# Splitting a small weight load, trimming warm-up matmuls and moving a loop's entry waits, in a matmul kernel that is bound by TensorE

## The chip, the cores and the metric

One Trainium2 chip, one core. The metric is the device time of one execution in microseconds (us), as the median of several executions. In the profile, PE is TensorE's matmuls, PEld its weight loads, PEldq and SPq the sequencers of TensorE and SyncE, DVE is VectorE, ACT ScalarE, POOL GpSimd. Moments are counted from the start of the profiled span. A profile is one execution; an execution's time is its span plus about 1.7 us.

## The reference

```python
# x: 1 x 384 x 384 x 384, dw: 1 x 1 x 384, pw: 384 x 384, all bfloat16
out = x * dw[0, 0]                       # the depthwise part, kernel size 1
return jnp.einsum('bhwc,cd->bhwd', out, pw)
```

So: 147,456 rows of 384 numbers, times one 384 x 384 matrix whose rows are scaled by dw.

## The kernel before

The kernel scales pw once and then multiplies. Rows are handled in 288 "supertiles" of 512 rows. For each, VectorE transposes X into T, TensorE runs 48 matmuls (four row groups of 32 at a time, so 12 sets of four), ScalarE copies the result out of PSUM, and DMA stores it. The TensorE program has a head, then a loop of 144 rounds of two supertiles.

The head works as follows. dw lands and goes through a matmul with a one to become a column (`dw_f`). VectorE scales a selection matrix by it (`sel_w`). TensorE multiplies `sel_w` with pw into PSUM (12 "weight matmuls", two for each of six blocks), and six copies, five on ScalarE and one on VectorE, bring the blocks to SBUF as `w_r`. Dummy matmuls on zeros (`idle_work`) keep TensorE busy meanwhile. The first supertile may not start before blocks 0, 2 and 3 are copied: its first matmul reads block 0, and blocks 2 and 3 lie in the PSUM banks that it writes.

```python
nc.scalar.dma_start(dw_row[:], ...).then_inc(s_dw, 16)
nc.sync.dma_start(pw_n[:], pw.rearrange("(k p) d -> p k d", p=P)).then_inc(s_pw, 16)
# ... then the loads of X and the stores, on the same SyncE queue

w_eng = [1, 0, 1, 1, 1, 1]            # block 1 is copied by VectorE, the others by ScalarE
# ... w_done[b] = (semaphore, value) that tells of block b's copy

def supertile(s, rv):
    for b in range(NB):
        for par in range(2):
            for q in range(4):
                if par == 0 and q == 0 and b in (0, 3):
                    nc.tensor.wait_ge(s_t[s][b // 3], rv)
                mm = nc.tensor.matmul(PS[s][:, q, :D], lhsT=Ts[s][...], rhs=w_r[...], ...)
                if b == 0 and par == 0 and q == 0:
                    mm._wait_ge(s_a[s], rv)
                elif s == 0 and q == 0 and par == 0:
                    mm._wait_ge(*w_done[b])
                # ...

def idle_work(n):
    with nc.tensor.Fori(0, n, 1) as _:
        for i in range(8):
            nc.tensor.matmul(PS[0][:, i % 4, :D], lhsT=zero[...], rhs=zero[...], ...)

nc.tensor.wait_ge(s_zero, 1)
idle_work(2)
nc.tensor.wait_ge(s_dw, 16)
# ... the dw matmul, three of one column
idle_work(2)
nc.tensor.wait_ge(s_pw, 16)
for b in range(NB):
    if b % 2 == 0:
        nc.tensor.wait_ge(s_sw, b // 2 + 1)
    # ... two weight matmuls
for b in (0, 2, 3):
    nc.tensor.wait_ge(*w_done[b])
with nc.tensor.Fori(0, NS // 2, 1) as it:
    rv = nc.tensor.to_reg(it + 1)
    for s in range(2):
        supertile(s, rv)
```

## Time and profile before

| | before |
|---|---|
| median, first three executions | 576.24 us (575.96 to 576.51) |
| profiled execution | 575.67 us, span 574.0 us |
| matmuls of the loop, first to last start | 561.46 us |
| head, to the first loop matmul | 7.44 us |
| tail, from the last matmul's start | 5.06 us |

The loop is a fixed quantity: 12 sets of four matmuls at 162.5 ns for each of 288 supertiles. Apart from one wait per round that moves inside the loop, all that the change touches is the head. The prediction below shows the lines.

### The profile page before, as it was taken

The page shows a single profiled execution, that of the slowest core. Times are in us where ns is not written, and L with a number is a line of the kernel's source. Part 1 is how long each engine was busy: PE and PEld are TensorE (multiplying, and loading weights), DVE is VectorE, ACT ScalarE, POOL GpSimd, SP SyncE. Part 2 cuts the span into 40 slices and gives each one's busy share as a digit, 9 for nine tenths or more (in the row PEclk, how much of TensorE's full clock was granted, in tenths as well). Part 3 has the DMA queues.
Part 4 walks back from the last instruction along what each step waited for, and adds up shares of the span by engine and source line. Part 5 has one row for each costly group of instructions (what it writes and reads, how often), then busy time and mean ns, then how long its engine had stood idle before and what let it go on. Part 6 is the DMA issues. An engine that isn't in the chain of part 4 may idle for free.

```text
span 574.0 us, 29707 instructions
## 1 busy us (share of the span) xinstructions
PE 566.9 (99%) x13871; PEld 415.2 (72%) x13871; DVE 507.4 (88%) x582; ACT 418.7 (73%) x296; POOL 1.7 (0%) x8
## 2 busy tenths in 40 slices
PE   8999999999999999999999999999999999999996
PEld 5777777777777777777777777777777777777774
DVE  6888988988898898889889888988988898899884
ACT  6777777777777777777777777777777777777775
POOL 1000000000000000000000000000000000000000
PEclk9999999999999999999999999999999999999999
DMA  8999999999999999999999999999999999994996
GB/s 340 431 404 412 429 417 427 436 423 419 380 408 413 392 388 431 398 392 392 431 397 394 390 436 396 398 392 426 403 382 421 411 385 397 413 400 153 411 403 244
DMA packets 25912, 226.88 MB, mean 395 GB/s; under 512 B 1197, under 2 KB 5678, under 8 KB 22062
## 3 DMA queue, kind: packets, MB, share of 16 engines
q1 hardware_dynamic: 25900, 226.79, 98.0%
q14 instruction: 9, 0.07, 0.0%
q8 instruction: 1, 0.02, 0.0%
q10 hardware_dynamic: 2, 0.00, 0.0%
HBM read 113.54 MB, written 113.25 MB: 395 GB/s over the span
## 4 chain that ended last, share of the span: by engine, by line
PE 98%; ACT 1%; DMA 0%; DVE 0%; issue 0%; POOL 0%; POOLq 0%; SPq 0%
PE ps L162 97%; PE ps L181 0%; DMA out_dram<-O 0%; ACT w_r L268 0%; ACT O L296 0%; DVE O L293 0%; PE ps L212 0%; POOL zero L229 0%; POOL warm L228 0%; POOLq L326 0%; PE ps L196 0%; SPq L99 0%
## 5 line engine op out<-in xcount | busy, mean ns | idle before, releaser
L162 PE MATMUL ps<-w_r,T 32*128 32x384 bf16 x13824 | 561.8, 321 | 0.9 <-ACT w_r L268 0.9
L255 DVE STREAM_TRANSPOSE T<-X 128x384 uint32<-128x384 uint32 x576 | 504.5, 878 | 55.8 <-DMA X<-in_x_dram 0.7
L296 ACT CAST O<-ps 128x1536 bf16<-128x1536 f32 x288 | 413.5, 1436 | 148.2 <-PE ps L162 148.2
L162 PEld LDWEIGHTS ps<-w_r,T 32*128 32x128 bf16 x13824 | 413.0, 93 | 149.6 <-issue 1.2
L268 ACT CAST w_r<-ps 128x768 bf16<-128x768 f32 x5 | 3.6, 820 | 1.7 <-PE ps L212 1.7
L181 PE MATMUL ps<-zero 32*128 32x384 bf16 x32 | 2.8, 516 | 1.4 <-POOL zero L229 1.4
L293 DVE CAST O<-ps 128x768 bf16<-128x768 f32 x1 | 1.0, 957 | 3.0 <-DMA out_dram<-O 3.0
L273 DVE COPY dw_f<-ps 128x3 f32<-128x3 f32 x1 | 0.2, 160 | 3.0 <-PE ps L196 3.0
L181 PEld LDWEIGHTS ps<-zero 32*128 32x128 bf16 x32 | 1.1, 118 | 2.0 <-issue 1.7
L212 PE MATMUL ps<-pw_n,sel_w 128*128 128x384 bf16 x12 | 2.4, 332 | 0.0
L241 ACT ACT_TABLE_LOAD x1 | 1.3, 1283 | 1.5 <-SPq L99 1.5
L212 PEld LDWEIGHTS ps<-pw_n,sel_w 128*128 128x128 bf16 x12 | 1.0, 99 | 1.7 <-DMA pw_n<-in_pw_dram 0.6
L268 DVE CAST w_r<-ps 128x768 bf16<-128x768 f32 x1 | 1.0, 957 | 0.9 <-PE ps L212 0.9
L277 DVE TENSOR_SCALAR sel_w<-sel,dw_f 128x512 bf16<-128x512 bf16 x3 | 0.9, 350 | 0.1
L231 POOL TENSOR_SCALAR_AFFINE_SELECT sel<-ones 128x512 bf16<-128x512 bf16 x1 | 0.7, 735 | 0.1
L196 PEld LDWEIGHTS ps<-ones,dw_row 1*128 1x128 bf16 x3 | 0.3, 127 | 0.3 <-issue 0.2
L230 POOL MEMSET ones<- 128x512 bf16 x1 | 0.5, 528 | 0.0
L241 ACT COPY warm<-warm 128x1 f32<-128x1 f32 x2 | 0.3, 189 | 0.0
L229 POOL MEMSET zero<- 128x192 uint32 x1 | 0.3, 257 | 0.0
L196 PE MATMUL ps<-ones,dw_row 1*128 1x1 bf16 x3 | 0.3, 174 | 0.0
L315 POOL MEMSET const-bfloat16-1.0<- 128x1 bf16 x1 | 0.1, 102 | 0.0
L315 POOL MEMSET const-uint8-127<- 128x1 uint8 x1 | 0.1, 102 | 0.0
(3 smaller groups left out, 0.3 us busy)
## 6 DMA issues: line engine op xcount, KB each, us to landing
X<-in_x_dram SPq DMA_DIRECT2D x26, 3840.0 KB, 21.1
out_dram<-O SPq DMA_DIRECT2D x26, 3840.0 KB, 27.1
X<-in_x_dram SPq DMA_DIRECT2D x2, 1536.0 KB, 17.1
out_dram<-O SPq DMA_DIRECT2D x2, 1536.0 KB, 13.7
X<-in_x_dram SPq DMA_DIRECT2D x3, 768.0 KB, 7.5
out_dram<-O SPq DMA_DIRECT2D x3, 768.0 KB, 9.8
X<-in_x_dram SPq DMA_DIRECT2D x1, 2304.0 KB, 18.7
out_dram<-O SPq DMA_DIRECT2D x1, 2304.0 KB, 11.7
```

The source lines that it names most:

```text
L162: mm = nc.tensor.matmul(PS[s][:, q, :D], lhsT=Ts[s][32 * q : 32 * q + 32, b, par::2], rhs=w_r[32 * q : 32 * q + 32, b, par, :], start=(b = ...
L181: nc.tensor.matmul(PS[0][:, i % 4, :D], lhsT=zero[32 * (i % 4) : 32 * (i % 4) + 32, 0:P], rhs=zero[32 * (i % 4) : 32 * (i % 4) + 32, :], s ...
L196: mm = nc.tensor.matmul(PS[1][:, k, D : D + 1], lhsT=dw_row[:, P * k : P * k + P], rhs=ones[0:1, 0, 0:1], start=True, stop=True,)
L212: mm = nc.tensor.matmul(w_ps(b)[:, r, :], lhsT=sel_w[:, b // 2, 2 * (b % 2) + r, :], rhs=pw_n[:, b // 2, :], start=True, stop=True,)
L230: nc.gpsimd.memset(ones[:], 1.0).then_inc(s_seed)
L231: nc.gpsimd.affine_select(out=sel[:].rearrange("p (v r) (q w) -> p v r q w", v=2, q=4), in_=ones[:].rearrange("p (v r) (q w) -> p v r q w" ...
L241: c = nc.scalar.copy(warm[:, s + 1 : s + 2], warm[:, 0:1])
L255: ins = nc.vector.transpose(out=Tw[:, 3 * h : 3 * h + 3], in_=Xw[:, :, j, 96 * h : 96 * h + 96].rearrange("p k (b w) -> p b k w", w=32),)
L268: i = nc.vector.tensor_copy(out, in_) if e == 0 else nc.scalar.copy(out, in_)
L277: nc.vector.tensor_scalar_mul(sel_w[:, k], sel[:], dw_f[:, k : k + 1]).then_inc(s_sw)
L293: e = nc.vector.tensor_copy(Ov[:, nq:4, j, :], PS[s][:, nq:4, :D])
L296: a = nc.scalar.copy(Ov[:, 0:nq, j, :], PS[s][:, 0:nq, :D])
```

## The change

Its intent: start the weight matmuls sooner, by letting the first third of pw land alone and by running less dummy work ahead of them; and start the loop sooner after the copies, by letting the loop be entered before they end.

```diff
-        nc.sync.dma_start(pw_n[:], pw.rearrange("(k p) d -> p k d", p=P)).then_inc(s_pw, 16)
+        nc.sync.dma_start(pw_n[:, 0, :], pw[:P, :]).then_inc(s_pw[0], 16)
+        nc.sync.dma_start(pw_n[:, 1:3, :], pw[P:, :].rearrange("(k p) d -> p k d", p=P)).then_inc(s_pw[1], 16)
...
+        w_first = {0: [(0, 1), (1, 3)], 4: [(1, 4)], 5: [(1, 5)]}
...
+                        if s == 0 and par == 0 and q == 0 and b in w_first:
+                            for e, v in w_first[b]:
+                                nc.tensor.wait_ge(s_wr[e], v)
...
-                        elif s == 0 and q == 0 and par == 0:
-                            mm._wait_ge(*w_done[b])
...
-                for i in range(8):
+                for i in range(4):
...
-        idle_work(2)
+        idle_work(4)
...
-        nc.tensor.wait_ge(s_pw, 16)
         for b in range(NB):
+            if b in (0, 2):
+                nc.tensor.wait_ge(s_pw[b // 2], 16)
...
-        for b in (0, 2, 3):
-            nc.tensor.wait_ge(*w_done[b])
```

## The prediction

> **What bounds the kernel now.** I read the page first (busy shares, chain by line, costliest groups), then the chain in order of time, then the timeline of the first eleven microseconds, then the loop's sequencer lines.
>
> ```profile
> PE 566.9 (99%) x13871; PEld 415.2 (72%) x13871; DVE 507.4 (88%) x582; ACT 418.7 (73%) x296; POOL 1.7 (0%) x8
> ...
> PE ps L162 97%; PE ps L181 0%; DMA out_dram<-O 0%; ACT w_r L268 0%; ACT O L296 0%; DVE O L293 0%; PE ps L212 0%; POOL zero L229 0%; POOL warm L228 0%; POOLq L326 0%; PE ps L196 0%; SPq L99 0%
> ...
> L162 PE MATMUL ps<-w_r,T 32*128 32x384 bf16 x13824 | 561.8, 321 | 0.9 <-ACT w_r L268 0.9
> ```
>
> In these page lines the reader is to see one thing: the matmuls of the loop (L162) are 97% of the chain, and over 13,824 of them the engine sat idle only 0.9 us, all of it before the first. 561.8 us / 13,824 x 4 = 162.5 ns for each set of four matmuls on the four row groups. There is nothing to win inside the loop but the matmuls themselves, and the change leaves their number alone. What is left is the part before the loop and the part after it.
>
> ```profile
> 1.43 1.46 PE ps L181 x15
> 2.89 0.03 PE ps L196
> 2.92 1.30 PE ps L181 x13
> 4.22 0.51 PE ps L212 x2
> 4.72 0.02 issue
> 4.75 2.21 ACT w_r L268 x3
> 6.96 0.48 issue
> 7.44 557.90 PE ps L162 x13728
> ```
>
> This is the chain in order of time: start, length, what. The loop starts at 7.44 us. Ahead of it: dummy matmuls (L181) until about 4.2, two weight matmuls (L212), three weight copies of ScalarE back to back (2.21 us), then 0.48 us of "issue", in which nothing that the profile shows was waited for. That 0.48 us is the change's main target.
>
> ```profile
> L221 PEldq EVENT_SEMAPHORE  x1: 51/51/51, 7.0 to 7.0; - x1
> ...
> L222 PEldq FUSED_REGOPS  x144: 35/35/44, 7.2 to 564.4; - x144
> L222 PEldq ALU_OP  x144: 36/36/36, 10.2 to 567.9; - x144
> L222 PEldq COMPARE_BRANCH  x144: 76/208/218, 10.3 to 568.0; - x144
> L222 PEldq MOVE  x1: 29/29/29, 7.1 to 7.1; - x1
> ...
> L161 PEldq EVENT_SEMAPHORE  x432: 51/51/51, 7.3 to 566.0; - x144
> ```
>
> These are the answers for lines 221, 222 and 161 (durations in ns min/median/max, then first and last start in us). Read in order of their first starts they are the 0.48 us: the wait for the copies ends at 7.0 (L221), then the loop counter's MOVE at 7.1, the loop's register operations at 7.2, the wait for the first transpose at 7.3 (L161), then the first weight load at 7.41 and the first matmul at 7.44. Setting up the loop comes **after** the wait, in series.
>
> ```profile
> 2.76 0.16 PE L196 MATMUL ps<-ones,dw_row 1*128 1x1 bf16 x1
> 2.78 1.44 PE L181 MATMUL ps<-zero 32*128 32x384 bf16 x13
> 4.15 0.40 PE L212 MATMUL ps<-pw_n,sel_w 128*128 128x384 bf16 x1
> ```
>
> And this timeline of PE before the copies shows what the other two parts aim at: the dummy matmuls run until 4.22 by their modelled end, and the first weight matmul starts at 4.15, put down by the profile to pw_n, whose landing is 3.0 us after its issue at 1.01, so about 4.0.
>
> **What the Trainium skill says.** (1) "TensorE: Matmul & The Clock Gate", section "Back-to-back issue gap": N/2.4 + 2.5 ns per warm matmul. For N = 384 this is 162.5 ns, exactly this trace's figure per set of four; so the loop is at its floor and a wait already satisfied costs nothing visible. (2) Same page, "Part 1: The HAM clock gate": cold, the array runs at half clock until about 3.4 us of activity, in a free-running window. The trace agrees: dummy matmuls last 522 ns against 321 in the loop, their sets follow at about 320 ns, and the first pair of L212 at 231 ns, which puts the switch near 4.3 us (231 ns = 142 at 1.2 plus 89 at 2.4 for 384 columns). (3) Same page, "Architectural detail": TensorE's queue is 64 deep. In the trace the loop-end ALU_OP runs at 10.2 while the next round's first matmul is due at 7.44 + 2 x 1.95 = 11.34: the sequencer is some 1.1 us ahead. (4) "DMA: Bandwidth & Descriptors", "Anatomy of one DMA": about 2 us fixed per transfer plus bytes over 436 GB/s. That is the fit of another issue path, but pw_n (288 KB) gives 2.0 + 0.7 = 2.7 against 3.0 measured, close enough to size a split.
>
> **The change part by part.**
>
> *pw in two transfers.* 96 KB is 0.22 us of data against 0.68, so the first third should land some 0.45 us sooner, about 3.5 instead of 4.0. The price is one more issue on the SP queue, 0.45 us by pw_n's own issue and 0.47 from each X issue to the next; every X load is issued that much later. X0 landed at 1.53 + 3.4 = 4.97 and is first used at 5.95, when VectorE has finished its weight copy: slack 1 us. X1 landed at 6.5 and is used at 7.34 (single instructions read from narrow windows of the timeline). The tightest later one is the 3840 KB load of supertile 10: the DMA engines are full from 3 us on, its transpose ended 25.78 and PE needed it at 26.94, slack 1.16 us. A loss of up to 0.5 us in landing and a loop 0.4 us earlier leave about 0.3. So the delay is hidden, though not by much.
>
> *Shorter dummy work.* 32 dummy matmuls become 24. But the first 16 are now four rounds of four instead of two rounds of eight. A cold set of four takes 0.32 us; a round trip of the loop took 0.44 us from the first weight load to the next round's (1.40 to 1.84). Four sets therefore start about 0.42 apart instead of 0.30 apart: the last near 2.68 instead of 2.34. The dw matmul (L196), which must wait its turn on row group 0, moves from 2.66 to about 2.68 + 0.32 = 3.0. Everything behind it shifts: the copy of dw (0.16), sel_w (0.35), first ready at 3.61 before, about 3.95 after. The second dummy loop is two sets, done by about 3.9. So the first weight matmul starts near 4.05 instead of 4.15, now released by sel_w and not by pw. Since the clock is still cold until about 4.3, of that 0.1 only about 0.03 reaches the second matmul's end, and ScalarE's copies start at 4.72 instead of 4.75. The copies stay back to back at 0.69 us; so I book **0.03 us** for the first two parts together.
>
> *Waits inside the loop.* In the built program the first matmul of the loop now has two wait instructions ahead of it (one for s_wr0, one that holds s_wr1 and the transpose) and one attached, and the copies' three waits ahead of the loop are gone. MOVE, branch and register operations now run while PE is idle anyway. What remains after the third copy is one wait instruction (released 29 ns after the update: 6.96 to 6.99), 76 ns to the weight load (7.33 to 7.41) and 31 ns to the matmul: 0.14 instead of 0.48. **0.34 us** gained. Is something else then last? The first transpose ended at 6.81, 0.15 ahead of the third copy; the second at 7.49 against a need at 8.1; copies 4 and 5 end at 7.65 and 8.36, needed at 7.1 + 4 x 0.325 = 8.4 and 8.7. All hold.
>
> In each of the other 143 rounds the wait instructions stay three in number: the one at block 3 goes away (its wait is now attached), one more stands at the loop's top. That adds about 0.1 us where the sequencer is already busy with the back edge: ALU_OP at 10.2, first pushes by about 10.9, first matmul due 11.34. A margin of 0.45 us shrinks to 0.35; nothing shows. The tail after the last matmul (569 to 574) is untouched.
>
> Sum: 0.34 + 0.03 = 0.37, so 576.24 - 0.4 = **575.8 us**.
>
> **The rivals.** *The loop's top becomes the limit.* If PE's queue ran dry at the back edge, each 10 ns would cost 144 x 10 = 1.4 us. Against it: 0.45 us of margin, and an extra 0.1. It would give 577 to 580; I hold it at 4%. *The clock.* Less dummy work may leave the array looking idle between 3.3 and 4.0, and the switch to full clock would fall a window later, at about 7.7. Then twelve weight matmuls run at 320 ns, the copies starve by a few tenths, the loop begins at about 7.6 and its first sets run at half speed: 576.5 to 577; were it missed twice, 578. For it: the window is free-running and the array had been busy since only 1.43. Against it: over 80% of the time up to 4.3 stays busy. 12%. *The X loads become the bound* at supertile 10: the gain of the loop's entry is given back by 0.1 to 0.3, 576.0. 12%. *The split of pw pays in full*: if the round trip of the shorter dummy loop costs less than I think, the first weight matmul starts at 3.7 and the chain gains 0.2 more: 575.6. 15%.
>
> **Range and chances.** All rivals but the first move the time by 0.3% or less, and the three runs of before already spread over 0.55 us. So 575.1 to 576.7 for 8 in 10. Faster by over 2% would need 11.5 us, more than the whole of what is not loop (574.0 - 561.8 = 12.2) could reasonably give: 1%. Slower by over 2% would need the loop's top to starve by 80 ns a round: 1%.
>
> **What would show it.** Right: the chain's "issue" before L162 falls from 0.48 to about 0.14; L196 starts later, near 3.0; the first copy of ScalarE starts within 0.1 of 4.75; L162 starts at about 7.07, its 13,824 matmuls still take 561.6 to 561.9 us, idle 0. Wrong: gaps over 140 ns between sets at the loop's top, a stall of L162 on T near 26 us, L212 matmuls all at 320 ns, or L212 starting before 3.9.

## The result and the profile after

| | before | after |
|---|---|---|
| median of the same rounds, 6 executions each | 576.51 us (575.96 to 578.79) | 576.08 us (575.63 to 576.22) |
| profiled execution | 575.67 us | 575.63 us |

The ratio is 0.9986, with a 95% interval of 0.9969 to 1.0002: the same within 2%, and by the times alone not even surely faster. (A ratio here is the mean time of one kernel's fast runs over that of the other's of the same rounds, so not quite the ratio of the medians.) The predicted 575.8 was 0.28 us low and its range holds the result.

The page of the changed kernel first: the loop's matmuls, with their busy time, the mean length in ns, and the engine's idle time before them.

```profile
L165 PE MATMUL ps<-w_r,T 32*128 32x384 bf16 x13824 | 561.8, 321 | 0.5 <-ACT w_r L268 0.5
```

Busy time in the loop is the same 561.8 us. The idle time before it fell from 0.9 to 0.5 us, as the last weight matmuls moved closer. Now the chain in order of time (start, length, what) of the changed kernel:

```profile
1.43 1.74 PE ps L182 x14
3.16 0.06 PE ps L197 x3
3.23 0.79 PE ps L182 x8
...
4.04 1.70 PE ps L214 x6
...
5.76 1.51 ACT w_r L268 x2
7.26 0.14 issue
7.40 557.90 PE ps L165 x13728
```

Two things changed against the chain of before. The "issue" ahead of the loop is 0.14 us instead of 0.48. But the copies end at 7.26 instead of 6.96, and the chain now runs through **six** weight matmuls and two copies, not two and three. ScalarE waited for the weight matmuls. So the loop starts at 7.40 instead of 7.44: in these two profiles the entry's gain of 0.34 was given back, all but 0.04, by something upstream.

The sequencer's lines at the loop's entry (durations in ns, then first and last start in us):

```profile
L164 PEldq EVENT_SEMAPHORE  x288: 51/51/51, 6.6 to 564.6; - x144
...
L222 PEldq FUSED_REGOPS  x144: 35/35/44, 6.5 to 564.4; - x144
...
L222 PEldq MOVE  x1: 29/29/29, 6.4 to 6.4; - x1
```

MOVE and the register operations run at 6.4 and 6.5, before the copies end at 7.26, and not after, as before. The timeline of PE before the copies:

```profile
3.02 0.21 PE L197 MATMUL ps<-ones,dw_row 1*128 1x1 bf16 x3
3.12 0.89 PE L182 MATMUL ps<-zero 32*128 32x384 bf16 x8
4.04 0.48 PE L214 MATMUL ps<-pw_n,sel_w 128*128 128x384 bf16 x1
```

The dw matmul at 3.02 and the first weight matmul at 4.04 are where the prediction put them (3.0 and 4.05). What is new is the length of that weight matmul: 0.48 us, where the first of before took 0.40 and the others 0.33. All twelve, as min/median/max in ns, of before, of the changed kernel, and of a run below with only the split (three answers on pw_n):

```profile
L212 PE MATMUL ps<-pw_n,sel_w x12: 323/326/396, 4.2 to 6.3; 128*128 128x384 bf16 x12
```
```profile
L214 PE MATMUL ps<-pw_n,sel_w x12: 326/326/524, 4.0 to 6.6; 128*128 128x384 bf16 x12
```
```profile
L214 PE MATMUL ps<-pw_n,sel_w x12: 326/448/524, 4.2 to 6.9; 128*128 128x384 bf16 x12
```

524 ns is the length at half clock (the dummy matmuls of before had 522), 326 that at full clock. Before, only the first of the twelve met the slow clock, and only in part; in the changed kernel's profile the first four did, and with only the split, seven. The trace's clock records put the switch at **4.31 us** before and at **5.18 us** after. The same records show the other end. This is the table of stretches past the last matmul, whose third column from the right is the granted clock, first of before and then of after:

```profile
571.00:572.00 1.00, 0.00 (x0) 0.00 (x0) 0.00 (x0) 0.00 (x0) 0.00 (x0) 1.00 0.87 341
```
```profile
571.00:572.00 1.00, 0.00 (x0) 0.00 (x0) 0.00 (x0) 0.00 (x0) 0.00 (x0) 0.90 0.92 362
572.00:573.00 1.00, 0.00 (x0) 0.00 (x0) 0.00 (x0) 0.00 (x0) 0.00 (x0) 0.50 0.09 31
```

After the last matmul the clock falls back to 0.50, in the changed kernel at 571.79 (0.90 in that microsecond is 0.79 at 1 and 0.21 at 0.5). From 5.18 to 571.79 are 566.61 us, 166.0 times 3.413 us; before, from 4.31 to 574.34 are 167.0 times the same. In all ten profiles of this document the two lie 166.0 or 167.0 times 3.413 us apart. So the switch happens on the ticks of a 3.413 us clock that runs on its own. The Trainium skill says just that ("TensorE: Matmul & The Clock Gate", section "Part 1: The HAM clock gate"): the window is 3413 ns and "it doesn't reset when your kernel starts".

### The profile page after: what moved, and what is told of

Same layout as the page of the kernel before. It is cut to its first block, busy times and chain, and to the rows that moved or that the text cites. A ratio compares the mean times of both kernels' runs of the same rounds, so it can differ in the third digit from the quotient of the medians.

```text
span 573.9 us, 29696 instructions
## 1 busy us (share of the span) xinstructions
PE 567.2 (99%) x13863; PEld 412.2 (72%) x13863; DVE 506.9 (88%) x582; ACT 418.9 (73%) x296; POOL 1.7 (0%) x8
## 4 chain that ended last, share of the span: by engine, by line
PE 98%; ACT 1%; DMA 0%; DVE 0%; issue 0%; POOL 0%; POOLq 0%; SPq 0%
PE ps L165 97%; PE ps L182 0%; DMA out_dram<-O 0%; PE ps L214 0%; ACT w_r L268 0%; ACT O L296 0%; DVE O L293 0%; POOL zero L229 0%; POOL warm L228 0%; PE ps L197 0%; POOLq L326 0%; SPq L99 0%
## 5 line engine op out<-in xcount | busy, mean ns | idle before, releaser
L165 PE MATMUL ps<-w_r,T 32*128 32x384 bf16 x13824 | 561.8, 321 | 0.5 <-ACT w_r L268 0.5
```

What stands on the lines that cost most here:

```text
L165: mm = nc.tensor.matmul(PS[s][:, q, :D], lhsT=Ts[s][32 * q : 32 * q + 32, b, par::2], rhs=w_r[32 * q : 32 * q + 32, b, par, :], start=(b = ...
```

## The experiments

The theories to tell apart:

- **A**: the gain at the entry is real, but the change's thinner dummy work made the clock switch late and gave it back.
- **B**: moving the waits only moved the time elsewhere; there is no gain.
- **C**: the split costs, through the later X loads.
- **D**: the gain at the entry is real, and the moment of the switch is chance, whatever the dummy work.

Each kernel was timed in 5 to 6 executions, one of them profiled, with the kernel before beside it on the same chip (576.51 us median in the rounds of the first four, 576.37 of the last four).

**Only the waits inside the loop** (the hunks on `w_first`, `w_done` and the loop over (0, 2, 3), on the kernel before).

> Only the third part of the change: the copies' waits stand inside the loop. Theory A (the entry gain is real and the head of the changed kernel gave it back because the clock switched late, at 5.18 us, after less dummy work): entry, third ScalarE copy to first loop matmul, 0.14 us instead of 0.49; first loop matmul near 7.10 where the clock switches by 4.3; time 0.35 us below before, 0.3 below the change when the clocks agree. Rival B (the change gained at the entry only what a moved wait took elsewhere): entry 0.14 but copies later, first loop matmul 7.4, time as before. Both: loop 561.46 us from first to last matmul.

Measured: 576.05 us median (575.49 to 578.55), ratio 0.9989 (0.9976 to 1.0003). Its profiled execution was its slowest, 578.55. The chain:

```profile
4.22 2.05 PE ps L212 x6
...
6.29 1.51 ACT w_r L266 x2
7.80 0.14 issue
7.93 561.80 PE ps L164 x13824
```

The entry is 0.14 again, with nothing else changed. But here, with the **full** dummy work of before, the clock switched at 6.57 and the copies ended at 7.79, later than in the changed kernel. That speaks against A. B's 7.4 is not met either, but later copies are what B forecast, so this run alone does not settle it: the entry gained 0.34 against the profile of before, while the copies lost 0.84, which the table below puts down to the clock. (The 2.4 us that made this execution the slowest lie in the tail: the last stores took 3.7 and 4.7 us to land, against 2.3 before. No edit touches the tail. Whether the other slow executions are slow for the same reason is not known, as they have no profile.)

**Only the split.**

> Only the first part: pw_n in two transfers. Theory A: first 96 KB lands near 3.0, but the dummy matmuls end and sel_w is ready no earlier than before, so the first weight matmul starts at 4.0 to 4.15, gain 0 to 0.1 us; X loads issued 0.4 us later, X0 lands near 5.5 and is not waited for. Rival C (the split itself costs): copies or the first transpose start later by 0.3 and the time is 0.3 us above before.

Measured: 576.47 us median (575.92 to 576.54), ratio 0.9996 (0.9983 to 1.001). pw's first part landed at 2.95 instead of 4.0, and the first weight matmul still started at 4.15, as the dummy matmuls stood ahead of it.

```profile
4.22 2.05 PE ps L214 x6
...
6.29 1.51 ACT w_r L270 x2
7.80 0.43 issue
8.23 561.81 PE ps L163 x13824
```

This chain and the one above are the same to 0.01 us up to the end of the copies, as both had a late clock (6.19 and 6.57). They differ in one step: 0.43 us of issue with the waits ahead of the loop, 0.14 with them inside. That is the cleanest measure of the third part: 0.30 us from loop start to loop start. B does not fit this pair, as the copies end at 7.79 in both. X0 landed at 5.6 and its transpose ended 0.85 us before the loop's start, so C is not seen.

**Only the dummy work.** (`range(4)`, `idle_work(4)` first.)

> Only the second part: dummy work in rounds of four, 24 instead of 32. Theory A: the dw matmul starts at 3.0 instead of 2.66, the first weight matmul near 4.05 to 4.15, and the clock switches later more often, so that the copies end 0.3 us later: time 0 to 0.5 us above before. Rival D (the time of the switch is chance, whatever the dummy work): time as before within 0.1, and the switch falls at other places from execution to execution in all four of these kernels alike.

Measured: 576.34 us median (576.24 to 576.63), ratio 0.9997 (0.9983 to 1.0011). The dw matmul moved to 3.01 and sel_w to 3.89, as expected, but pw landed at 4.13, later than either, so the weight matmuls began at 4.18, 0.03 later than before. The switch came at 5.91. Time as before.

**The change with the dummy work of before.**

> The change with the dummy work of before put back. Theory A: dw matmul at 2.66, first weight matmul 4.0 to 4.15, entry 0.14, first loop matmul near 7.05 to 7.1 where the clock switches by 4.3; time 0.3 to 0.5 us below the change (575.6 to 575.8). Rival D: same as the change, 576.0, as the late clock is chance.

Measured: 576.14 us median (575.5 to 576.2), ratio 0.9988 (0.9975 to 1.0002). Switch at 6.08, third copy at 7.77, entry 0.14, first loop matmul at 7.91. Theory A wanted 575.6 to 575.8; D wanted the changed kernel's time and got it.

**The dw matmul as soon as dw lands.** The four runs above say what paces the weight matmuls of the changed kernel: not pw, which is there at 3.0, but sel_w at 3.9, which hangs on a dw matmul that queues behind sixteen dummies. So:

```diff
         def idle_work(n):
-            with nc.tensor.Fori(0, n, 1) as _:
+            for j in range(n):
...
-        idle_work(4)
+        idle_work(2)
```

> The change, with the dummy work cut to two sets of four ahead of the dw matmul and two after it, written out without loops. Theory D (the switch of the clock is chance; sel_w, which waits for the dw matmul, paces the weight matmuls): the dw matmul runs when dw lands, near 2.26 instead of 3.0, sel_w is ready near 3.1, the first weight matmul starts at 3.15 to 3.25, 0.8 to 0.9 us earlier than in the change; the third ScalarE copy ends at 6.9 even with a late clock, the first loop matmul is near 7.05; median time 575.2 to 575.5. Theory A (less dummy work delays the clock): the switch comes after 7 us, and the time is 0.5 us or more above the change.

Measured: **575.51 us** median (575.3 to 575.74), ratio 0.9985 (0.9972 to 0.9998). The head of its chain:

```profile
0.97 1.35 DMA dw_row<-in_dw_dram
...
2.91 0.36 DVE sel_w L277
...
3.41 1.99 PE ps L214 x6
...
6.93 0.14 issue
7.07 561.81 PE ps L165 x13824
```

The dummies are off the chain. The dw matmul ran at 2.36, when dw had landed (0.1 later than expected), sel_w was ready at 3.26, and the weight matmuls began at 3.41 instead of 4.04. The switch was at 5.16, as late as in the changed kernel's first profile (5.18), yet the loop starts 0.33 us earlier, 7.07 against 7.40. All five executions lie below 575.75. This version beats both kernels: in its rounds every execution of before took 575.79 or more, and every one of the changed kernel (the repeat below) 576.04 or more. Against before it is 0.9 us (means 575.50 and 576.40), about 0.15%.

**No dummy work at all.** (`idle_work(0)` twice, on the version above.)

> As the one above with no dummy matmul at all. Theory D as far as it goes: first weight matmul near 3.15, copies as there; the clock switches later than 5 us in most executions, as there is less work in the window, so the first sets of the loop may run at half speed: 575.2 to 576.5. Theory A: switch at 7.5 to 9, the weight matmuls all at 320 ns and the first sets of the loop too, 577 or more.

Measured: 575.76 us median (575.31 to 577.63, with 576.68 the next), ratio 0.9996 (0.9983 to 1.0008). By chance dw landed 0.33 us later in the profiled execution (2.65), so the weight matmuls began at 3.76, not near 3.15; the clock switched at 6.58, the loop began at 7.52. Half of its executions are as fast as the version with dummies, two are much slower. Their profiles don't exist, so whether the clock or a late store made them slow stays open. Theory A's 577 or more is not the rule here.

**The early version without the split.**

> The early version with pw_n again in one transfer. If the split pays only once sel_w is no longer the later of the two: pw_n lands at 4.0 to 4.1, the first weight matmul starts at 4.05 to 4.15 and the first loop matmul 0.8 us later than in the early version, time 0.5 to 0.9 above it. If the split is worth nothing even then: the same as the early version.

Measured: 576.61 us median (575.91 to 578.37), ratio 1.0009 (0.9997 to 1.0021). pw landed at 3.85 and the first weight matmul started at 3.89, 0.48 us later than with the split: now pw is the last to come. The loop began at 7.75 instead of 7.07. Not all of that is the split, for the clock switched only at 7.59 in this execution, every weight matmul was slow, and the last of them, not the third copy, was what the loop waited for. So, at the first weight matmul: the split is worth 0.48 us once sel_w comes early, 0.14 with the change's own dummy work (4.18 without the split, 4.04 with it), and nothing with the dummy work of before (4.15 both).

**The changed kernel again.**

> The changed kernel once more. Theory D: the same program shows another moment of the clock's switch, anywhere from 4.3 to 7.7 us, and with it the end of the third copy, 6.9 (early) to 7.8 (late), first loop matmul 0.14 us after; times spread over 575.5 to 576.3. Theory A (the switch belongs to the program): 5.2 us again, third copy 7.26.

Measured: 576.05 us median (576.04 to 577.83), ratio 1.0002 (0.9989 to 1.0015). The same program, another moment: the clock switched at 6.02 instead of 5.18, and the third copy ended at 7.65 instead of 7.26. Theory A would have had 5.18 again. And it was not the copies that came last this time:

```profile
1.92 4.92 DMA X<-in_x_dram
...
6.87 0.87 DVE T L255
7.74 0.09 issue
7.83 561.81 PE ps L165 x13824
```

X0 took 4.92 us to land, and the first transpose ended at 7.73, 0.07 after the third copy. The early version without the split had the same, 4.93 us, there without harm; the other eight profiles, with and without the split, had 3.4 to 3.8. So the slow landing does not go with the split. But that it came last here does: with two transfers of pw ahead of it, X0 is issued at 1.92 instead of 1.53, and 0.39 us sooner would have ended the transpose about 0.3 us ahead of the third copy (an estimate, with the same time to land). So C's cost is likely real in this one execution, though under 0.1 us.

All ten profiles together (moments in us; "entry" is from the end of the third ScalarE copy to the first loop matmul):

| kernel | dummies | first weight matmul | clock switch | third copy ends | waits | entry | first loop matmul |
|---|---|---|---|---|---|---|---|
| before | 32 | 4.15 | 4.31 | 6.95 | ahead of the loop | 0.49 | 7.44 |
| only waits | 32 | 4.15 | 6.57 | 7.79 | inside | 0.14 | 7.93 |
| only split | 32 | 4.15 | 6.19 | 7.79 | ahead | 0.44 | 8.23 |
| only dummies | 24 | 4.18 | 5.91 | 7.70 | ahead | 0.44 | 8.14 |
| waits and split | 32 | 4.15 | 6.08 | 7.77 | inside | 0.14 | 7.91 |
| the change | 24 | 4.04 | 5.18 | 7.26 | inside | 0.14 | 7.40 |
| the change again | 24 | 4.04 | 6.02 | 7.65 | inside | 0.17 | 7.83 |
| early | 16 | 3.41 | 5.16 | 6.92 | inside | 0.14 | 7.07 |
| early, no split | 16 | 3.89 | 7.59 | 7.53 | inside | 0.22 | 7.75 |
| no dummies | 0 | 3.76 | 6.58 | 7.38 | inside | 0.14 | 7.52 |

The four rows with the first weight matmul at 4.15 are the proof for the clock: up to there they are alike, and the end of the third copy goes with the switch, 6.95 for 4.31 and 7.77 to 7.79 for anything past 6.0. At full clock, two weight matmuls take 2 x 0.162 = 0.32 us and ScalarE, at 0.69 us a copy, is the slower; at half clock they take 0.64, and since VectorE's block 1 stands between blocks 0 and 2, ScalarE waits up to 0.5 us for its second copy; the first, too, begins up to 0.26 us later. That is a loss of up to 0.84 us, more than twice the 0.30 to 0.34 of the entry.

Is the moment of the switch all chance, as D says? Where the ticks fall is. But each trace also has a tick 3.413 us before its switch, which was passed over. In nine profiles it lies between 0.90 and 3.17, with at most 1.73 us of matmuls in the 3.41 us before it. In the early version without the split it lies at 4.18. Here is PE's busy time in the 3.41 us before that tick, and before the tick at 4.31 that switched the clock in before (second number):

```profile
0.77:4.18 3.41, 2.01 (x20) 1.00 0.60 189
```
```profile
0.90:4.31 3.41, 2.88 (x36) 1.00 0.59 198
```

(The granted clock of 1.00 in these two lines is no reading: the records begin with the switch.) Every tick with 2.01 us or less was passed over; every tick with 2.82 (no dummies, at 6.58) or more switched the clock. For the changed kernel this answers A: its passed ticks, at 1.77 and 2.60, had 0.34 and 1.18 us behind them, and the head of before, busy since the same 1.43, would have had no more. For the early version without the split it does not: with the full dummy work 2.75 us would have lain before 4.18, so its thinner dummy work may well have cost it that tick, and 7.59 is then not chance alone. No run tested this.

## Why the prediction was right, and where it was not

- **The loop is at its floor.** Right: 561.46 us from the first to the last matmul in all ten profiles, to 0.003.
- **The entry, 0.48 to 0.14.** Right to 0.01 us in the changed kernel. Against kernels measured with the waits ahead of it, it is 0.30 rather than 0.34 (0.44 in the two experiments, 0.49 in before). The 0.05 between them lies between the end of the last wait and the loop counter's MOVE, 0.10 us in before and 0.05 in the two; why is not shown.
- **The extra wait at the loop's top is hidden.** Right: in the second round the two waits ran at 10.67 and 10.86, the round's first matmul was due at 11.30, and no set in the loop came late.
- **The dummy loop of four delays the dw matmul to 3.0, sel_w to 3.95, the first weight matmul to 4.05.** Right: 3.02, 3.89, 4.04. The two head parts of the change work against each other: one brings pw 1.0 us sooner, the other brings sel_w 0.3 us later, and the later of the two counts.
- **The first third of pw lands at 3.5.** Off: at 3.02, 2.0 us after its issue. The estimate from the fit of the skill, 2.0 us plus bytes, was 0.2 too high for this size and the 0.5 subtracted from pw's own 3.0 too small. It changed nothing, as sel_w came later.
- **The X loads stay hidden, with 0.3 us left at supertile 10.** Right, with more room: 0.66 us in the changed kernel; the second issue moved X0's by 0.39 us, not 0.45. But X0 itself came last once, in the repeat, after a landing of 4.92 us, which the prediction, with its slack of 1 us, did not foresee.
- **The step that failed: the clock "still cold until about 4.3", hence "ScalarE's copies start at 4.72 ... the copies stay back to back", booked as 0.03 us of gain.** Measured in the changed kernel: first copy at 4.87, second only at 5.76, third ending 0.31 later than before. The prediction had the window's free run from the skill, and still took the one switch in the profile of before for a property of the kernel. It named the late clock as a rival, but as one window later (7.7) at 12%; in fact the ten switches are spread from 4.31 to 7.59, and the last of them, one tick after a passed one at 4.18, is that rival come true in another kernel.
- **The sum.** 576.24 - 0.4 = 575.8 against 576.08 measured, and the difference to before of the same rounds is 0.43 us. That the medians differ by what was predicted is partly luck, since executions of one kernel scatter by as much; the interval of the ratio still reaches 1, and the repeat gave 1.0002, as one of its five executions took 577.83. In the two profiles themselves the loop starts only 0.04 us sooner. What is shown is the step of 0.30 to 0.34 us at the entry, in every profile with the waits inside in which the third copy came last. The medians agree with it: 576.05 to 576.14 for only the waits, the waits and split, and the change twice, and 576.34 to 576.51 for before, only the split and only the dummies. The two other parts alone give ratios of 0.9996 and 0.9997.

A last point on the reading. The profile of before that everything was worked out from was its luckiest: 575.67 us, under each of the other executions of before (575.76 to 578.79), and its clock switched earliest of all ten, at 4.31. A typical execution at 576.4 is 0.7 us longer, which, if its tail is the same, puts its first loop matmul near 8.15 (an estimate); the two experiments that kept the old entry had 8.14 and 8.23.

## What to carry to other kernels

Put a wait where the wait is needed, not ahead of a loop's entry: here 0.3 us of loop set-up moved into time in which TensorE's sequencer had nothing else to do, and a satisfied wait inside the loop cost nothing over 144 rounds. When several things must be there before work can start, speeding one helps only until the next one is last: the split of pw gave 0, 0.14 or 0.48 us, depending on how early the dummies and sel_w let the weight matmuls start. And before a head of a few microseconds is tuned from one profile, look at a second one: the clock's switch falls on a tick whose place the kernel does not set, and a head that is robust to a late switch (work begun earlier) is worth more than one that is shorter in a lucky run.

## What the Trainium skill lacked or had wrong

- "TensorE: Matmul & The Clock Gate", "Part 1: The HAM clock gate": borne out, with numbers it does not have. The up-switch and the fall-back lie 166.0 or 167.0 ticks of 3.413 us apart in every trace, and the switch came 2.9 to 6.2 us after the first matmul of the head. The page puts the variation at about 500 ns either way; four programs here that are alike up to the first weight matmul have it from 4.31 to 6.57, 2.3 us apart. The page does not say how much of a window must be busy: here 2.01 of 3.41 us was not enough and 2.82 was. It does not say that the fall-back at the end of a trace tells the phase of the window, which the granted clock past the last matmul shows.
- Same page, "Back-to-back issue gap": the isolated formula N/2.4 + 2.5 ns gives 162.5 ns for 384 columns, and this is the pitch of four matmuls on four row groups, 1950 ns for 12 sets, with each matmul's own weight load hidden. The page says that real streams of weight load and matmul stay above the formula at 128 columns and below it at 512; it has no figure for 384 columns or for sets on four row groups, where the formula holds for the set.
- "Advanced Engine Details and Errata", "Control Flow Timing": about 108 ns for a compare-and-branch. Here the record of one taken in the main loop is mostly 207 or 208 ns, of the one not taken 76 ns, and a round trip of a short loop on TensorE, from the first weight load to the next round's, cost 0.38 to 0.44 us.
- "DMA: Bandwidth & Descriptors", "Anatomy of one DMA": the fit is for the other issue path. Here 96 KB landed 1.9 to 2.0 us after the issue, against 2.2 by the fit, and the same 384 KB load of X0 took 3.4 to 3.8 us to land in eight profiles and 4.9 in two, with programs that don't differ in what stands ahead of it in a way that would sort them.
